# The sign of converted weights from a Prelu on ScalarE instead of a VectorE pass, and a new place for the conversions

## The chip, the cores and the metric

The kernel runs on one core of one Trainium2 chip. The core has five engines that work at the same time, each through its own instructions in order: TensorE (PE, matrix products), VectorE (DVE), ScalarE (ACT), GpSimd (POOL) and SyncE (SP, which here only starts transfers). Sixteen DMA engines move data between the chip's memory and the core's SBUF. The metric is the device time of one execution in microseconds (us). The kernel before takes 677.11 us (median of three runs, 675.74 to 677.26).

## The reference

Two stages follow each other. The first is a recurrence over time (RWKV-6 attention) on 4 sequences of 768 tokens with 8 heads of width 48; the second is a dense layer of 3072 tokens, 384 to 2048 to 384 features, with the activation h - tanh(h).

```python
for t in range(S):                      # 768 steps, per batch and head
    cur = np.einsum('bhd,bhe->bhde', u[None] * kt, vt)
    y[:, :, t] = np.einsum('bhd,bhde->bhe', rt, state + cur)
    state = wt[:, :, :, None] * state + np.einsum('bhd,bhe->bhde', kt, vt)
# ... y to (B*S, H*D) = x
h = x @ w_in
g = h - np.tanh(h)
return g @ w_out
```

The two weight matrices arrive as 64-bit floats (the division by a 64-bit root makes them so), and the kernel turns them into 32-bit floats on the chip, from the two 32-bit words of each number.

## The kernel before

The tokens are worked in eight blocks of 384. Each block's dense layer has 16 tiles of 128 features (`f` = 0 to 15): TensorE makes `hp` from `xT` and the tile's first weights, ScalarE makes six tiles from it, VectorE makes `g` from those, and three iterations later (`LAG = 3`) TensorE adds `g` times the tile's second weights to `acc`. While block i goes through its tiles, the attention of block i+1 is worked in between, a phase at a time. The attention of block 0 has nothing to hide behind; it is the "boot".

The weights are sixteen tiles as well (768 KB each as 64-bit numbers), and each must be loaded into one of five `raw` buffers and converted before its `hp`. The conversion in the kernel before has two activations on ScalarE and three passes on VectorE:

```python
UPSCALE = 2.0 ** 8
HIGH_SCALE = 2.0 ** -111
RAWS = 5                                 # buffers of the pool conv
# ...
    def load_weights(f, queue):
        raw = conv.tile([P, 2 * DM, 2], I32, name="raw", tag="raw")
        ins = queue.dma_start(out=raw, in_=weights[f].bitcast(I32).rearrange("p (n two) -> p n two", two=2))
        return f, raw, ins

    def convert(f, raw, _):
        lo, hi = raw[:, :, 0], raw[:, :, 1]
        a = w_sb[:, f, :].bitcast(I32)
        up = conv.tile([P, 2 * DM], I32, name="up", tag="up", bufs=3)
        nc.scalar.activation(out=a.bitcast(F32), in_=hi.bitcast(F32), func=AF.Copy, scale=HIGH_SCALE)   # L167
        nc.scalar.activation(out=up, in_=lo.bitcast(U32), func=AF.Copy, scale=2.0 ** -29)              # L168
        return [
            lambda: nc.vector.tensor_single_scalar(a, a, 3, op=ALU.logical_shift_left),                # L170
            lambda: nc.vector.scalar_tensor_tensor(out=a, in0=hi, scalar=-2 ** 31, in1=a,              # L171
                                                   op0=ALU.bitwise_and, op1=ALU.bitwise_or),
            lambda: nc.vector.tensor_tensor(out=a, in0=a, in1=up, op=ALU.add)]                         # L173
```

The high word, read as a 32-bit float, is scaled by 2^-111. That moves its exponent so that a shift of the bits by three to the left puts the exponent and the mantissa of the 64-bit number where a 32-bit float has them. The shift pushes the sign out, so L171 takes it from the high word again. L173 adds the upper bits of the low word.

In the boot ScalarE starts the conversions of weights 0 to 2 early. The rest of it, from the last level of the attention on, stands in this order:

```python
        converted()                                   # VectorE passes of weight 0
        for p0 in HALVES:
            blk.turn(ps, p0)                          # transposes (L340), copies ks (L342)
        for copies in last:
            copies()                                  # ScalarE copies (L328)
        begin_behind(blk.update(ps, h1), later.load("kq", kT, 0, NPAIR))   # products L358, states L369
        blk.update(ps, h2)
        ready.append(convert(*raws.pop(0)))           # weight 3 on ScalarE
        blk.result(ps, [h1, h1 + 1])                  # products L389, L407, copies to xT (L420)
        blk.fill_holes([nc.sync, nc.scalar])
        more_weights(nc.sync)                         # load of weight 5
        later.mix(0, NPAIR, ("kmix",))                # ScalarE (L220)
        blk.result(ps, [h2, h2 + 1], True)
        later.load("rp", rT, 0, NPAIR)
        converted()                                   # weight 1
        more_weights(nc.sync)                         # load of weight 6
        later.load_v()
        for _ in range(2):
            ready.append(convert(*raws.pop(0)))       # weights 4 and 5 on ScalarE
        while ready:
            converted()                               # weights 2 to 5
            if ready:
                more_weights(nc.gpsimd)               # loads of weights 7 to 9
```

During block 0 (i = 0) a plan says in which iteration each attention phase of block 1, each conversion and each load stands. The VectorE passes of a conversion come one iteration after its ScalarE part, placed between the last passes of that iteration's `g`:

```python
            steps = (1, 2, 3, 4, 5, 7, 9, 10, 12)     # level 1, 2, 4, 8, 16, 32, turn, update, result
            before = {0: ("totals 1", "totals 2", "kq")}
            behind, converted = {1: ("rp",)}, (0, 3, 4, 4, 6, 9, 9, 10, 11, 11)
            loads = {1: "weights", 2: "weights", 5: "weights", 6: "weights", 7: "weights", 8: "weights",
                     9: "rmix", 10: "kmix", 11: "wt", 13: "kq", 14: "rp", 15: "v"}
# ... the loop over the tiles of a block
        for f in range(NF):
            g, next_rest = first(here, f, ps_d)       # hp on TensorE (L467), six ScalarE steps (L474-L479)
            waiting.append((second, f, g))
            for n, op in enumerate(rest):             # VectorE: g of the tile before (L484, L489, L492)
                op()
                if n >= 2 and extra:
                    extra.pop(0)()                    # VectorE passes of conversions
            for op in extra:
                op()
            # ... attention phase of block i+1, loads
            extra = []
            for _ in range(converted.count(f)):
                extra += convert(*raws.pop(0))
            if len(waiting) > LAG:
                s, fs, gs = waiting.pop(0)
                s.add(fs, gs)                         # acc on TensorE (L505)
```

`hp` has one buffer: the product of the next tile waits until ScalarE's step h (L474) has read it. An attention level's products (L240) need the decays of kq and rp of the level before, two VectorE passes (L272).

Of the kernel before, what the change touches and what calls it, by code (L numbers as in the profile page):

```python
# [37 lines left out]
F32 = mybir.dt.float32  # L38
# [4 lines left out]
AF = mybir.ActivationFunctionType  # L43
ALU = mybir.AluOpType
# [10 lines left out]
NPAIR = H // 2  # L55
# [22 lines left out]

UPSCALE = 2.0 ** 8
HIGH_SCALE = 2.0 ** -111  # L80


@with_exitstack
def kernel(
# [10 lines left out]
    nc = tc.nc  # L95
# [58 lines left out]

    def load_weights(f, queue):
        raw = conv.tile([P, 2 * DM, 2], I32, name="raw", tag="raw")
        ins = queue.dma_start(out=raw, in_=weights[f].bitcast(I32).rearrange("p (n two) -> p n two", two=2))
        return f, raw, ins  # L160

    def convert(f, raw, _):

        lo, hi = raw[:, :, 0], raw[:, :, 1]
        a = w_sb[:, f, :].bitcast(I32)
        up = conv.tile([P, 2 * DM], I32, name="up", tag="up", bufs=3)
        nc.scalar.activation(out=a.bitcast(F32), in_=hi.bitcast(F32), func=AF.Copy, scale=HIGH_SCALE)  # L167
        nc.scalar.activation(out=up, in_=lo.bitcast(U32), func=AF.Copy, scale=2.0 ** -29)  # L168
        return [
            lambda: nc.vector.tensor_single_scalar(a, a, 3, op=ALU.logical_shift_left),  # L170
            lambda: nc.vector.scalar_tensor_tensor(out=a, in0=hi, scalar=-2 ** 31, in1=a,  # L171
                                                   op0=ALU.bitwise_and, op1=ALU.bitwise_or),
            lambda: nc.vector.tensor_tensor(out=a, in0=a, in1=up, op=ALU.add)]  # L173


# [338 lines left out]
    def plan(i):  # L514

        names = ("level 1", 2, 4, 8, 16, 32, "turn", "update", "result")
        if i == 0:

            steps = (1, 2, 3, 4, 5, 7, 9, 10, 12)
            before = {0: ("totals 1", "totals 2", "kq")}  # L520
            behind, converted = {1: ("rp",)}, (0, 3, 4, 4, 6, 9, 9, 10, 11, 11)
            loads = {1: "weights", 2: "weights", 5: "weights", 6: "weights", 7: "weights", 8: "weights",
                     9: "rmix", 10: "kmix", 11: "wt", 13: "kq", 14: "rp", 15: "v"}
        else:
            steps = (4, 5, 6, 7, 8, 9, 10, 11, 13)
            before = {0: ("kmix",), 1: ("rmix",), 2: ("totals 1",), 3: ("totals 2", "kq"), 4: ("rp",)}
            behind, converted = {}, ()
            loads = {5: "rmix", 7: "kmix", 9: "wt", 11: "kq", 14: "rp", 15: "v"}
        return dict(zip(steps, names)), before, behind, converted, loads
# [3 lines left out]
    raws = []  # L533

    def more_weights(queue):
        raws.append(load_weights(more_weights.n, queue))
        more_weights.n += 1
        return raws[-1][-1]
# [3 lines left out]
    def begin_behind(ins, dma):  # L542


        tc.add_manual_dep(dma.ins, ins.ins.name, mybir.DependencyInfo(
            mybir.DependencyClass.Sync, mybir.DependencyReason.DATA))

    def boot(ps, blk, later):

        h1, h2 = HALVES  # L550
        for p0 in HALVES:
            for name, src in (("kq", kT), ("rp", rT), ("wt", wT)):
                blk.load(name, src, p0, UP)
        for name in ("rmix", "kmix"):
            blk.tiles[name] = inp.tile([P, NPAIR * NB], F32, name=name, tag=name)
        more_weights(nc.sync)
        blk.load_v()
        for _ in range(2):
            more_weights(nc.sync)
        blk.mix(h1, UP, copy=nc.vector.tensor_copy)  # L560
        masked = blk.level_1(ps, h1)
        blk.decay(1, h1, UP)
        blk.totals(1, h1, UP)
        blk.mix(h2, UP, copy=nc.scalar.copy)
        masked()
        blk.level(ps, 2, h1, UP)
        masked = blk.level_1(ps, h2)
        blk.decay(1, h2, UP)
        blk.totals(1, h2, UP)
        for m in (2, 4, 8, 16):  # L570
            blk.totals(m, h1, UP)
        masked()
        background = [lambda: later.load("rmix", rT, 0, NPAIR), lambda: later.load("kmix", kT, 0, NPAIR),
                      lambda: later.load("wt", wT, 0, NPAIR)] + [lambda: more_weights(nc.sync)] * 2
        ready, last = [], []
        for m in (2, 4, 8, 16, 32):
            for p0 in HALVES:
                if (m, p0) != (2, h1):
                    ins = blk.level(ps, m, p0, UP, last)
                if p0 == h2 or m == 32:  # L580
                    blk.totals(m, p0, UP)
            begin_behind(ins, background.pop(0)())
            if m <= 8:
                ready.append(convert(*raws.pop(0)))
            if m == 8:
                later.mix(0, NPAIR, ("rmix",))

        def converted():
            for op in ready.pop(0):
                op()  # L590

        converted()
        for p0 in HALVES:
            blk.turn(ps, p0)
        for copies in last:
            copies()
        begin_behind(blk.update(ps, h1), later.load("kq", kT, 0, NPAIR))
        blk.update(ps, h2)
        ready.append(convert(*raws.pop(0)))
        blk.result(ps, [h1, h1 + 1])  # L600
        blk.fill_holes([nc.sync, nc.scalar])
        more_weights(nc.sync)
        later.mix(0, NPAIR, ("kmix",))
        blk.result(ps, [h2, h2 + 1], True)
        later.load("rp", rT, 0, NPAIR)
        converted()
        more_weights(nc.sync)
        later.load_v()
        for _ in range(2):
            ready.append(convert(*raws.pop(0)))  # L610
        while ready:
            converted()
            if ready:
                more_weights(nc.gpsimd)

    with tc.tile_pool(name="ps_boot", bufs=4, space=PSUM) as ps_boot:
        xT = blocks[0].begin()
        boot(ps_boot, blocks[0], blocks[1])
# [3 lines left out]
    for i, blk in enumerate(blocks):  # L622
        here = xT
        later = blocks[i + 1] if i + 1 < len(blocks) else None
        after = blocks[i + 2] if i + 2 < len(blocks) else None
        if later:
            xT = later.begin()
        phases, before, behind, converted, loads = plan(i)
        second = Second(blk.b * S + blk.q * NB, ps_d)
        for f in range(NF):  # L630
# [82 lines left out]
```

## Time and profile before

| what | value |
|---|---|
| time, median of 3 | 677.11 us |
| span of the profiled execution | 677.3 us |
| TensorE busy | 642.3 us (95%) |
| VectorE busy | 559.3 us (83%) |
| ScalarE busy | 488.7 us (72%) |
| conversions, ScalarE (L167, L168) | 14.6 and 14.6 us for 16 each |
| conversions, VectorE (L170, L171, L173) | 9.0, 15.3 and 15.2 us for 16 each |
| loads of raw weights | 13 by SyncE, 3 by GpSimd, 768 KB each |

The busy shares are averages over the whole span. The conversions all lie in the first 126 us of it: the VectorE pass L171 has its first start at 30.6 us and its last at 124.9 us. The profile also has a view of windows, which gives the busy time of each engine in a stretch:

```profile
40.00:50.00 10.00, 7.06 (x59) 3.98 (x58) 8.80 (x11) 7.94 (x15) 1.74 (x3) 0.56 0.84 306
50.00:60.00 10.00, 4.97 (x104) 3.15 (x103) 8.38 (x17) 5.84 (x12) 0.00 (x0) 0.78 0.82 324
130.00:140.00 10.00, 10.00 (x32) 5.89 (x31) 9.38 (x19) 7.72 (x16) 0.00 (x0) 1.00 0.43 156
```

Each line has a stretch and its length, then the busy time of TensorE, of its weight loads, of VectorE, ScalarE and GpSimd with the number of instructions, the granted TensorE clock as a share of full speed, the DMA engines' busy share and the GB/s they moved. In 50 to 60 us TensorE is busy for half the time and its clock is on average at 0.78; in 130 to 140 us it has no gap at all.

### The profile page before, as it was taken

The numbers are of one execution on the slowest core, as the hardware profiler recorded it, in microseconds if no ns is written. First come the engines' busy times: TensorE is split into PE (matmuls) and PEld (weight loads), VectorE is DVE, ScalarE is ACT, GpSimd is POOL, SyncE is SP. The second block draws the span as 40 slices with busy tenths as digits, with TensorE's granted clock in tenths as the row PEclk, the third lists the DMA queues.
The fourth block names the chain that finished last, engine by engine and source line by source line (L and its number), as shares of the span: only waits on it lengthen the run. The fifth ranks groups of instructions, "written<-read, shape, count | busy, mean of one in ns | idle before, by whom it ended". The sixth has DMA issues, their size and how long they took to land.

```text
span 677.3 us, 19991 instructions
## 1 busy us (share of the span) xinstructions
PE 642.3 (95%) x8480; PEld 411.3 (61%) x8480; DVE 559.3 (83%) x1117; ACT 488.7 (72%) x966; POOL 5.2 (1%) x20
## 2 busy tenths in 40 slices
PE   4866899999999999999999999999999999999997
PEld 4743566566665666656666666656666566655554
DVE  7898999999986997689985998769986899747664
ACT  4575889885777758686676858677577857768874
POOL 2010000000000000000000000000000000000000
PEclk9967999999999999999999999999999999999999
DMA  8775152404012401124012130025011200000000
GB/s 311 236 253 215 49 179 104 137 36 143 5 47 90 147 32 49 24 94 150 3 47 92 39 140 23 28 90 176 4 48 49 79 2 3 3 10 35 1 1 36
DMA packets 30842, 54.38 MB, mean 80 GB/s; under 512 B 2336, under 2 KB 28704, under 8 KB 30752
## 3 DMA queue, kind: packets, MB, share of 16 engines
q1 hardware_dynamic: 30080, 50.46, 22.0%
q0 software_dynamic: 432, 2.36, 0.8%
q8 instruction: 67, 1.10, 0.7%
q10 hardware_dynamic: 240, 0.27, 0.1%
q14 instruction: 23, 0.19, 0.1%
HBM read 47.19 MB, written 4.72 MB: 77 GB/s over the span
## 4 chain that ended last, share of the span: by engine, by line
PE 71%; DVE 14%; issue 4%; PEld 4%; DMA 3%; ACT 3%; PEldq 1%; SPq 0%; DVEq 0%
PE acc L505 31%; PE hp L467 28%; PE att L240 8%; DVE states L369 2%; DMA raw<-in_weights 2%; PE att L407 2%; DVE hs L484 2%; PE att L340 2%; PEld hp L467 2%; PEld att L389 1%; DVE rp L272 1%; DVE gT L484 1%; DVE kq L272 1%; DVE w_sb L173 1%; DVE gT L492 1%
## 5 line engine op out<-in xcount | busy, mean ns | idle before, releaser
L467 PE MATMUL hp<-xT,w_sb 128*128 128x384 f32 x768 | 273.2, 493 | 8.9 <-ACT h L474 5.7
L505 PE MATMUL acc<-w_sb,gT 128*128 128x384 f32 x768 | 273.8, 493 | 0.0
L467 PEld LDWEIGHTS hp<-xT,w_sb 128*128 128x128 f32 x768 | 147.0, 192 | 113.0 <-ACT h L474 7.0
L505 PEld LDWEIGHTS acc<-w_sb,gT 128*128 128x128 f32 x768 | 140.5, 190 | 88.7 <-ACT o L510 2.3
L474 ACT ACTIVATE h<-hp 128x384 f32<-128x384 f32 x128 | 62.7, 490 | 144.9 <-PE hp L467 144.3
L489 DVE TENSOR_TENSOR th<-h,th 128x384 f32<-128x384 f32 x128 | 70.8, 553 | 43.9 <-ACT th L478 43.9
L484 DVE SCALAR_TENSOR_TENSOR hs<-h,s 128x384 f32<-128x384 f32 x128 | 70.9, 554 | 25.7 <-ACT s L475 25.7
L492 DVE COPY_PREDICATED gT<-big,th 128x384 f32<-128x384 int32 x128 | 76.1, 595 | 12.5
L476 ACT ACTIVATE qa<-s,shift 128x384 f32<-128x384 f32 x128 | 78.8, 615 | 4.2
L484 DVE SCALAR_TENSOR_TENSOR gT<-qb,hs 128x384 f32<-128x384 f32 x128 | 71.4, 558 | 9.4
L479 ACT ACTIVATE big<-s,shift 128x384 f32<-128x384 f32 x128 | 76.8, 600 | 0.0
L477 ACT ACTIVATE qb<-s,shift 128x384 f32<-128x384 f32 x128 | 76.7, 600 | 0.0
L484 DVE SCALAR_TENSOR_TENSOR hs<-qa,hs 128x384 f32<-128x384 f32 x128 | 70.4, 550 | 0.0
L475 ACT ACTIVATE s<-h 128x384 f32<-128x384 f32 x128 | 67.0, 523 | 4.1
L240 PEld LDWEIGHTS att<-rp,kq 48*64 48x64 f32 x3072 | 53.5, 145 | 25.1 <-issue 13.3
L240 PE MATMUL att<-rp,kq 48*64 48x32 f32 x3072 | 57.3, 229 | 8.1 <-DVE rp L272 5.5
L478 ACT ACTIVATE th<-h 128x384 f32<-128x384 f32 x128 | 64.9, 507 | 0.0
L272 DVE TENSOR_TENSOR kq<-kq,tot 128x768 f32<-128x768 f32 (+1 forms) x45 | 38.6, 858 | 4.0 <-PE att L240 2.6
L272 DVE TENSOR_TENSOR rp<-rp,tot 128x768 f32<-128x768 f32 (+1 forms) x45 | 38.8, 862 | 0.0
L369 DVE SCALAR_TENSOR_TENSOR states<-states,tot,att 128x48 f32<-128x48 f32 x176 | 31.5, 258 | 6.1 <-PE att L358 6.1
L300 DVE COPY_PREDICATED scores<-mask_all,att 128x384 f32<-128x384 uint8 (+1 forms) x54 | 31.9, 657 | 0.0
L240 PE MATMUL att<-rmix,kmix 48*64 48x64 f32 x768 | 14.5, 232 | 6.9 <-ACT rmix L220 6.9
(55 smaller groups left out, 352.1 us busy)
## 6 DMA issues: line engine op xcount, KB each, us to landing
raw<-in_weights SPq DMA_DIRECT2D x13, 768.0 KB, 4.6
rmix<-in_rT SPq DMA_DIRECT2D x7, 768.0 KB, 5.2
kmix<-in_kT SPq DMA_DIRECT2D x7, 768.0 KB, 6.8
wt<-in_wT SPq DMA_DIRECT2D x7, 768.0 KB, 7.7
kq<-in_kT SPq DMA_DIRECT2D x7, 768.0 KB, 4.5
rp<-in_rT SPq DMA_DIRECT2D x7, 768.0 KB, 4.7
v_sb<-in_v SPq DMA_DIRECT2D x8, 576.0 KB, 5.6
out_y<-o SPq DMA_DIRECT2D x23, 192.0 KB, 1.9
```

Of the source, the lines that this page charges most:

```text
L240: nc.tensor.matmul(dst, lhsT=lhs[rows, t0:t0 + L], rhs=src, start=True, stop=True)
L272: ins = nc.vector.tensor_tensor(out=part, in0=part, in1=by, op=ALU.mult)
L467: nc.tensor.matmul(hp, lhsT=w_in_sb[:, f, kc, :], rhs=xT[:, kc, :], start=(kc == KC - 1), stop=(kc == 0))
L475: nc.scalar.activation(out=s, in_=h, func=AF.Square)
L476: nc.scalar.activation(out=qa, in_=s, func=AF.Square, bias=shift[:, 0:1])
L477: nc.scalar.activation(out=qb, in_=s, func=AF.Square, bias=shift[:, 1:2])
L478: nc.scalar.activation(out=th, in_=h, func=AF.Tanh)
L479: nc.scalar.activation(out=big, in_=s, func=AF.Relu, bias=shift[:, 2:3])
L484: return lambda: nc.vector.scalar_tensor_tensor(out=out, in0=in0, scalar=scalar, in1=in1, op0=op0, op1=ALU.mult)
L489: lambda: nc.vector.tensor_tensor(out=th, in0=h, in1=th, op=ALU.subtract),
L492: lambda: nc.vector.copy_predicated(out=g, mask=big.bitcast(I32), data=th)]
L505: nc.tensor.matmul(acc, lhsT=g[:, j * P:(j + 1) * P], rhs=w_out_sb[:, f, :], start=(f == 0), stop=(f == NF - 1))
```

## The change

The sign comes from ScalarE. The first activation of a conversion becomes a Prelu with slope -2^32 for negative inputs: a positive number goes through as before; a negative one comes out positive and 2^32 times larger. That is a change of 32 in the exponent field, and the shift by three to the left carries this bit into the place of the sign. VectorE's pass L171 is left out. So VectorE no longer reads the raw words: a raw buffer is free when ScalarE's two activations have read it.

The conversions move too. In the boot the VectorE passes of weight 0 stand behind the updates of the state instead of ahead of them, weight 3 is converted after the transfers into the holes of xT, and the scaling of kmix moves ahead of the updates. Weights 7 to 10 are loaded in the boot by SyncE (7 to 9 were loaded by GpSimd, 10 in block 0). In block 0 the attention phases from level 16 on stand one iteration later, and the conversions are spread anew.

```diff
+NEGATIVE = -2.0 ** 32
...
-        nc.scalar.activation(out=a.bitcast(F32), in_=hi.bitcast(F32), func=AF.Copy, scale=HIGH_SCALE)
+        nc.scalar.activation(out=a.bitcast(F32), in_=hi.bitcast(F32), func=AF.Prelu,
+                             scale=HIGH_SCALE, alpha=NEGATIVE)
...
             lambda: nc.vector.tensor_single_scalar(a, a, 3, op=ALU.logical_shift_left),
-            lambda: nc.vector.scalar_tensor_tensor(out=a, in0=hi, scalar=-2 ** 31, in1=a,
-                                                   op0=ALU.bitwise_and, op1=ALU.bitwise_or),
             lambda: nc.vector.tensor_tensor(out=a, in0=a, in1=up, op=ALU.add)]
...
-            steps = (1, 2, 3, 4, 5, 7, 9, 10, 12)
+            steps = (1, 2, 3, 4, 6, 8, 10, 11, 13)
-            behind, converted = {1: ("rp",)}, (0, 3, 4, 4, 6, 9, 9, 10, 11, 11)
-            loads = {1: "weights", 2: "weights", 5: "weights", 6: "weights", 7: "weights", 8: "weights",
+            behind, converted = {1: ("rp",)}, (0, 3, 3, 4, 4, 6, 10, 10, 12, 13)
+            loads = {2: "weights", 5: "weights", 6: "weights", 7: "weights", 8: "weights",
...
-        converted()
         for p0 in HALVES:
             blk.turn(ps, p0)
         for copies in last:
             copies()
+        later.mix(0, NPAIR, ("kmix",))
         begin_behind(blk.update(ps, h1), later.load("kq", kT, 0, NPAIR))
         blk.update(ps, h2)
-        ready.append(convert(*raws.pop(0)))
         blk.result(ps, [h1, h1 + 1])
         blk.fill_holes([nc.sync, nc.scalar])
+        converted()
+        ready.append(convert(*raws.pop(0)))
         more_weights(nc.sync)
-        later.mix(0, NPAIR, ("kmix",))
+        converted()
         blk.result(ps, [h2, h2 + 1], True)
         later.load("rp", rT, 0, NPAIR)
-        converted()
         more_weights(nc.sync)
         later.load_v()
         for _ in range(2):
             ready.append(convert(*raws.pop(0)))
         while ready:
             converted()
-            if ready:
-                more_weights(nc.gpsimd)
+            more_weights(nc.sync)
```

## The prediction

> **What bounds the kernel now.** I read the busy shares first, then the forty slices, then the chain of waits of the first 72 us, and last the timelines of TensorE, ScalarE and VectorE there. TensorE is busy 95% of the span. From 118.60 us to the end it is busy 550.98 of 558.70 us, so nothing that ends after 118.60 us can give much, and the change touches nothing there. Before 118.60 us TensorE has gaps, and all sixteen weight conversions lie there: six of their VectorE parts before 50 us, ten between 56 and 125 us. The chain of waits shows what sets the pace in the middle of this stretch (start, length, what):
>
> ```profile
> 42.04 13.77 DMA raw<-in_weights
> 55.81 0.02 issue
> 55.84 0.90 ACT w_sb L167
> ...
> 57.79 0.87 DVE w_sb L171
> 58.66 0.06 DVE gT L492
> 58.72 0.33 issue
> 59.05 0.95 DVE w_sb L173
> 60.00 1.82 DVE scores L247 x2
> 61.82 0.84 DVE rp L272
> ```
>
> A weight load issued at 42.04 us lands 13.77 us later. ScalarE, which works in order, sits in front of the conversion of weight 6 until then, and the step h of the next dense tile stands behind it. Then VectorE carries the chain, with the sign pass (L171) in it. TensorE's timeline shows the price in brackets:
>
> ```profile
> 44.32 4.21 PE L467 MATMUL hp<-xT,w_sb 128*128 128x384 f32 x6 [2.19 <-ACT xT L420]
> 49.17 2.20 PE L467 MATMUL hp<-xT,w_sb 128*128 128x384 f32 x6 [0.64 <-ACT h L474]
> 51.30 1.63 PE L240 MATMUL att<-rmix,kmix 48*64 48x64 f32 x96
> 57.95 4.21 PE L467 MATMUL hp<-xT,w_sb 128*128 128x384 f32 x6 [5.03 <-ACT h L474]
> 62.76 1.60 PE L240 MATMUL att<-rp,kq 48*64 48x32 f32 x96 [0.60 <-PE hp L467]
> 64.29 2.20 PE L467 MATMUL hp<-xT,w_sb 128*128 128x384 f32 x6
> 67.20 1.60 PE L240 MATMUL att<-rp,kq 48*64 48x32 f32 x96 [0.71 <-DVE rp L272]
> ...
> 73.31 1.60 PE L240 MATMUL att<-rp,kq 48*64 48x32 f32 x96 [0.45 <-DVE rp L272]
> ...
> 80.53 1.60 PE L240 MATMUL att<-rp,kq 48*64 48x32 f32 x96 [1.55 <-DVE rp L272]
> ...
> 90.44 1.01 PE L317 MATMUL att<-rp,kq 48*32 48x32 f32 x96 [0.37 <-DVE rp L272]
> ...
> 109.34 2.17 PE L467 MATMUL hp<-xT,w_sb 128*128 128x384 f32 x6 [1.09 <-ACT qb L477]
> ```
>
> Each dense tile's hp is six records. It takes 2.1 to 2.2 us at the full clock and 4.21 us at the half clock. From the first second-layer product, at 68.73 us, to 118.60 us the gaps are 0.45 + 1.55 + 0.37 + 1.09 = 3.46 us. In 60 to 120 us VectorE is busy 98%: it is the bound of block 0, TensorE a close second. The pieces of a conversion (mean ns after the comma):
>
> ```profile
> L171 DVE SCALAR_TENSOR_TENSOR w_sb<-raw,w_sb 128x768 int32<-128x768 int32 x16 | 15.3, 956 | 0.3
> L173 DVE CUSTOM_DVE_ANT_0 w_sb<-w_sb,up 128x1536 uint16<-128x1536 uint16 x16 | 15.2, 952 | 1.2
> L167 ACT ACTIVATE w_sb<-raw 128x768 f32<-128x768 f32 x16 | 14.6, 911 | 7.9 <-DMA raw<-in_weights 7.8
> L170 DVE TENSOR_SCALAR w_sb<-w_sb 128x768 int32<-128x768 int32 x16 | 9.0, 560 | 2.0 <-ACT w_sb L167 2.0
> ```
>
> [...] So Prelu should take the 911 ns of Copy. The trace agrees for its other functions of one form (h 490, th 507, s 523 ns at 384 columns), and the built program of the change has, like the kernel before, one table load (1283 ns in the trace, at 0.82 us)[...]. [...] idle from 52.93 us, the clock reads 0.91 in 54 to 56 us and 0.50 in 56 to 62 us. [...] three loads issued by GpSimd at 41.55, 44.15 and 47.33 us share the engines with those of SyncE, and a 768 KB SyncE load takes 13.77 us here against a median of 4.6 us.
>
> **The change part by part.** (a) It removes sixteen L171 passes. Started back to back, an instruction costs its spacing and not its duration: in the boot the conversions follow each other every 2.55 us (36.82, 39.37, 41.93), and without L171 it should be 1.5 us (0.59 from shift to next, then 0.87). Inside block 0 an L171 costs 0.87 us when interleaved, 1.1 us in a bare sequence. So six times 1.05 = 6.3 us in the boot and ten times about 0.9 = 9 us in block 0 leave VectorE. Most of it cannot be cashed in, so I follow the path.
>
> (b) The first conversion moves from ahead of the state updates to behind them. It lay at 30.02 to 32.6 us, and the first update began at 32.61 us. But TensorE's update products start only at 31.54 us and their first half needs 0.9 us, so updates begin no earlier: 0 us. The end of the updates stays at 36.8 us.
>
> (c) On ScalarE the kmix scaling (1.56 us) and the conversion of weight 3 (1.7 us) change places. The second group of xT copies, which releases the first hp, starts about 0.2 us later, so hp starts at about 44.55 us for 44.32 us: +0.2 us. It is again at the half clock, ending at 48.75 us.
>
> (d) VectorE's boot conversions now wait for ScalarE. ScalarE gives weight 3 at 42.6 us and, after the xT copies, 4 and 5 at 46.2 and 47.8 us. VectorE ends the last at 48.7 us instead of 50.35 us, though 6.3 us of work is gone: it idles for the rest. Then totals (2.61 us), the kq decay (0.87 us) and the first dense chain, from 52.2 us instead of 53.83 us.
>
> (e) The loads of weights 7 to 9 move from GpSimd to SyncE, behind weight 6. Ahead of weight 6 are then only weight 5 and rp. Three 0.786 MB loads at the 0.40 to 0.43 MB/us seen between 46 and 56 us take 5.5 to 6 us from 42 us[...]. ScalarE finishes tile 0's six steps at 51.9 us, so it converts weight 6 at once instead of at 55.84 us. A raw buffer is also free after ScalarE's two reads, so no later load waits for VectorE.
>
> (f) Then h of tile 1 is at 53.55 us instead of 57.43 us, and hp of tile 2 at 54.05 us instead of 57.95 us. TensorE has then been idle about 1.1 us, not 5, so it should stay at the full clock. VectorE: dense chain 0 with the two conversion passes from 52.2 to 55.9 us, L247 to 57.7 us, rp decay to 58.55 us; chain 1 starts there and not at 62.57 us. Adding 2.4 us for chain 1 and 1.74 us for the level 2 decays gives 62.7 us, when the products that began at 67.20 us can begin; the first second-layer product follows at 64.4 us instead of 68.73 us: **4.3 us** gained.
>
> (g) After that, by iteration of block 0 (PE: hp 1.95, acc 1.95, attention 1.0 to 1.7; VectorE: chain 2.35, conversion 1.33, decays 1.74, masked copy 0.93). Iterations 4 and 5 carry two conversions each, 7.7 and 5.0 us of VectorE work against 5.6 and 4.0 us of TensorE work, but the two iterations after them have slack and level 16 and 32 moved one later, to 6 and 8. I find the decays of level 4 done at 68.5 us, when TensorE arrives, and those of level 8 at 76.2 us against an arrival at 78.1 us. ScalarE, with two conversions (3.25 us) in 3, 4 and 10, arrives in time by 0.1 to 0.6 us. So TensorE should become the bound, and the 3.46 us of gaps go: **3.5 us**. Sum 7.8 us; I keep 0.2 us for new small gaps. 677.1 - 7.6 = **669.5 us**.
>
> **The rivals.** *VectorE sets everything:* all 15 us off a nearly full engine would come off the time, 662 us. Against it: (d) leaves VectorE waiting for ScalarE, and TensorE's own idle time from 57.95 to 118.60 us is 60.65 - 55.78 = 4.9 us; with the 3.9 us of (f) and 2.1 us of half clock the ceiling is about 11 us. *Nothing reaches the end:* if weight 6 still lands late, since the same bytes cross the same engines, (f) fails and only the 3.5 us and part of 1.6 us remain: 673 us. Against it stands the order of the loads; for it, the 13.77 us. *ScalarE takes over:* it is busy 98% in 100 to 120 us and the change takes nothing from it. If Prelu cost 0.1 us more, or the two conversions at 10 delay h, gaps of 1 to 2 us come back: 671 us. *The clock drops again:* TensorE waits some 2.4 us at 56.1 us for the rp decay; if that makes it cold, hp costs 2.1 us more: 671.5 us.
>
> **Range and chances.** The rivals that cost lie 1.5 to 3.5 us above 669.5 us, the ones that gain are limited by 11 us, that is 666 us. Range 667 to 672.5 us. A gain of over 2% needs under 663.6 us, below the ceiling: 0.03. A loss of 2% would need a new wait of 20 us: 0.01. Within 2%: 0.96.
>
> **What would show it.** The L171 group gone and the conversion activation still near 911 ns; no wait for the load before weight 6 and hp of tile 2 near 54 us at 2.1 us; the first L505 product near 64.4 us; the bracketed gaps of L240 after it under 0.3 us; after 118.6 us nothing but a shift. It is wrong if ScalarE still waits for weight 6, if hp of tile 2 takes 4.2 us, or if waits for h of over 1 us appear in iterations 10 to 14.

## The result and the profile after

| | median | range | runs |
|---|---|---|---|
| before | 677.18 us | 675.74 to 677.65 us | 4 |
| after | 671.54 us | 671.01 to 673.00 us | 4 |

The ratio is 0.9924 with a 95% interval of 0.9902 to 0.9945: 5.6 us less, inside the 2% that counts as the same. Measured again later beside other kernels, the changed kernel had 672.34 us against 676.99 us, a ratio of 0.9931 (0.9917 to 0.9945). The prediction was 669.5 us, range 667.0 to 672.5 us. The profiled execution has a span of 669.7 us; VectorE's busy time went from 559.3 to 545.4 us, ScalarE's from 488.7 to 488.8 us. Lines of the kernel after lie two or three below those of before: hp is L469, the first conversion activation L170.

The chain of waits of the kernel after, in the stretch where before a weight load of 13.77 us stood:

```profile
50.58 0.51 ACT big L481
51.09 0.83 ACT w_sb L170
...
53.15 2.22 PE hp L469 x6
55.36 2.62 issue
57.98 2.79 PE att L242 x96
60.77 3.87 PE hp L469 x6
```

No transfer stands ahead of the conversion of weight 6 any more: ScalarE goes from the last step of tile 0 (`big`) straight into it, and hp of tile 2 starts at 53.15 us for 57.95 us. But further down there is a hole of 2.62 us, then an attention product of 2.79 us and an hp of 3.87 us. TensorE's timeline over the same time:

```profile
53.15 2.20 PE L469 MATMUL hp<-xT,w_sb 128*128 128x384 f32 x6 [0.88 <-ACT h L476]
57.98 2.79 PE L242 MATMUL att<-rp,kq 48*64 48x32 f32 x96 [2.63 <-issue]
60.70 3.94 PE L469 MATMUL hp<-xT,w_sb 128*128 128x384 f32 x6
64.58 1.60 PE L242 MATMUL att<-rp,kq 48*64 48x32 f32 x96
66.11 2.20 PE L507 MATMUL acc<-w_sb,gT 128*128 128x384 f32 x6
...
70.17 1.60 PE L242 MATMUL att<-rp,kq 48*64 48x32 f32 x96
...
117.09 0.36 PE L409 MATMUL att<-scores,v_sb 64*48 64x64 f32 x9 [0.74 <-issue]
```

The first second-layer product starts at 66.11 us (68.73 us before), and from there to 120 us only one gap of 0.74 us is left of 3.46 us; the product at 70.17 us, for example, waits for nothing. The windows of the kernel after give the granted clock (third number from the end) beside the busy times:

```profile
56.00:58.00 2.00, 0.02 (x3) 0.05 (x3) 2.00 (x4) 1.94 (x5) 0.00 (x0) 0.86 0.98 412
58.00:60.00 2.00, 2.00 (x76) 2.00 (x80) 1.86 (x5) 0.72 (x2) 0.00 (x0) 0.50 0.17 64
...
62.00:64.00 2.00, 2.00 (x4) 1.01 (x3) 2.00 (x3) 0.00 (x0) 0.00 (x0) 0.50 0.00 0
64.00:66.00 2.00, 2.00 (x98) 1.43 (x96) 1.97 (x5) 1.25 (x3) 0.00 (x0) 0.94 0.03 8
```

The clock falls inside the hole and comes back only at about 64.2 us (an estimate from the 0.94, with the half clock before and the full clock after): what runs between takes longer, the attention product 2.79 us for 1.60 us and hp of tile 3 3.94 us for 2.20 us. VectorE's timeline says what the hole waited for, which the chain calls "issue":

```profile
32.48 4.29 DVE L371 SCALAR_TENSOR_TENSOR states<-states,tot,att 128x48 f32<-128x48 f32 x24 [3.05 <-PE att L360]
...
44.72 0.56 DVE L174 TENSOR_SCALAR w_sb<-w_sb 128x768 int32<-128x768 int32 x1 [1.68 <-ACT w_sb L170]
...
56.94 0.94 DVE L274 TENSOR_TENSOR rp<-rp,wt 128x768 f32<-128x768 f32 x1
...
61.70 0.95 DVE L274 TENSOR_TENSOR rp<-rp,tot 128x768 f32<-128x768 f32 x1
```

The rp decay ends at 57.88 us and the product starts at 57.98 us. The next decay ends at 62.65 us; its product starts at 64.58 us, when TensorE at half clock has got there. The groups of the conversion:

```profile
L172 ACT ACTIVATE up<-raw 128x768 int32<-128x768 uint32 x16 | 14.7, 917 | 0.0
L170 ACT ACTIVATE w_sb<-raw 128x768 f32<-128x768 f32 x16 | 14.6, 911 | 7.0 <-DMA raw<-in_weights 4.1 <-issue 2.7
```

The Prelu (L170) takes 911 ns, to the nanosecond what the Copy took. Comparing the start of every hp in both traces gives the balance: tile 2 is 4.80 us earlier, tile 4 2.62 us, the end of block 0 5.15 us. Between that point and the last products some 1.1 us more come from small stalls, and 1.4 us of the 7.6 us between the two spans lie in the last store; that these two parts belong to the change is not shown.

### The profile page after: what moved, and what is told of

Read it like the earlier page. It is cut to its first block, busy times and chain, and to the rows that moved or that the text cites. A ratio compares the mean times of both kernels' runs of the same rounds, so it can differ in the third digit from the quotient of the medians.

```text
span 669.7 us, 19951 instructions
## 1 busy us (share of the span) xinstructions
PE 642.5 (96%) x8480; PEld 412.5 (62%) x8480; DVE 545.4 (81%) x1101; ACT 488.8 (73%) x966; POOL 3.5 (1%) x17
## 4 chain that ended last, share of the span: by engine, by line
PE 81%; PEld 4%; issue 4%; DVE 4%; ACT 3%; DMA 2%; PEldq 1%; SPq 0%; ACTq 0%; DVEq 0%
PE acc L507 34%; PE hp L469 33%; PE att L242 9%; DVE states L371 2%; PE att L409 2%; PEld hp L469 2%; PE att L342 2%; PEld att L391 2%; PE att L319 1%; PEld acc L507 1%; DMA wt<-in_wT 1%; DMA xT<-late 1%; PEldq L397 0%; ACT qb L479 0%; ACT h L476 0%
## 5 line engine op out<-in xcount | busy, mean ns | idle before, releaser
L469 PE MATMUL hp<-xT,w_sb 128*128 128x384 f32 x768 | 272.4, 492 | 4.0 <-DMA xT<-late 2.5
L469 PEld LDWEIGHTS hp<-xT,w_sb 128*128 128x128 f32 x768 | 147.0, 192 | 107.7 <-ACT h L476 3.4
L476 ACT ACTIVATE h<-hp 128x384 f32<-128x384 f32 x128 | 62.7, 490 | 143.5 <-PE hp L469 142.8
L242 PE MATMUL att<-rp,kq 48*64 48x32 f32 x3072 | 58.8, 231 | 6.5 <-issue 4.4
L274 DVE TENSOR_TENSOR kq<-kq,tot 128x768 f32<-128x768 f32 (+1 forms) x45 | 38.6, 859 | 4.2 <-PE att L242 2.3
L274 DVE TENSOR_TENSOR rp<-rp,tot 128x768 f32<-128x768 f32 (+1 forms) x45 | 38.8, 862 | 0.0
```

What stands on the lines that cost most here:

```text
L242: nc.tensor.matmul(dst, lhsT=lhs[rows, t0:t0 + L], rhs=src, start=True, stop=True)
L274: ins = nc.vector.tensor_tensor(out=part, in0=part, in1=by, op=ALU.mult)
L469: nc.tensor.matmul(hp, lhsT=w_in_sb[:, f, kc, :], rhs=xT[:, kc, :], start=(kc == KC - 1), stop=(kc == 0))
```

## The experiments

Three questions: is it the Prelu or the new order that pays; is the half clock after 57.4 us what was lost against the prediction; and is there more to be had once that is gone. None of these kernels leaves out a part of the computation.

| kernel | median us | before, same batch | ratio (95%) |
|---|---|---|---|
| Prelu alone | 673.48 | 677.57 | 0.9934 (0.9915 to 0.9954) |
| order and loads alone | 681.75 | 677.57 | 1.0062 (1.0043 to 1.0082) |
| after, loads by GpSimd | 674.83 | 677.57 | 0.9950 (0.9932 to 0.9969) |
| after, four fillers | 671.24 | 677.57 | 0.9902 (0.9882 to 0.9921) |
| after, conversions spread | 671.94 | 676.90 | 0.9916 (0.9891 to 0.9941) |
| after, totals into the hole | 670.07 | 676.90 | 0.9889 (0.9861 to 0.9916) |
| spread, totals, two fillers | 670.22 | 676.90 | 0.9886 (0.9862 to 0.9910) |
| the same, holes of xT by one queue | 670.03 | 676.90 | 0.9884 (0.9858 to 0.9911) |
| after again | 672.34 | 676.99 | 0.9931 (0.9917 to 0.9945) |
| after, fillers in two places | 670.67 | 676.99 | 0.9904 (0.9888 to 0.9920) |
| all together | 670.35 | 676.99 | 0.9897 (0.9879 to 0.9916) |
| after, weight 0 placed back | 672.37 | 676.99 | 0.9930 (0.9915 to 0.9944) |

**The Prelu alone.** The kernel before with only the conversion changed:

```diff
-  ... in_=hi, func=AF.Copy, scale=HIGH_SCALE)
+  ... in_=hi, func=AF.Prelu, scale=HIGH_SCALE, alpha=NEGATIVE)
-  lambda: nc.vector.scalar_tensor_tensor(out=a, in0=hi, scalar=-2 ** 31, ...)
```

> The kernel before with only the sign moved to Prelu and the VectorE pass left out; order, plan and loads as before. Theory A (a raw buffer is free as soon as ScalarE has read it, so weight 6 need not share the engines with three late loads, and VectorE has 15 us less to do; the new order adds little): weight 6 is there before 52 us, the gaps of TensorE after 66 us shrink, 671 to 673 us. Rival B (the new order of the boot and of block 0 and the loads on SyncE bring the gain, the pass was hidden): ScalarE still waits 3 to 4 us for weight 6, 675 to 677 us.

Measured: 673.48 us, 0.9934, half a us above the range of theory A; the ratios of the whole change (0.9924 and 0.9931) lie inside this interval, so that the new order and loads add anything is not shown. In the traces hp of tile 15 starts at 122.61 us here, 123.30 us in the kernel after and 128.44 us before. One reason is in GpSimd's timeline. First the kernel before, then the one with the Prelu alone; both issue the same three loads:

```profile
41.55 0.69 POOL L159 DMA_DIRECT2D raw<-in_weights  x1 [37.37 <-DVE w_sb L171]
44.15 0.53 POOL L159 DMA_DIRECT2D raw<-in_weights  x1 [1.91 <-DVE w_sb L171]
47.33 0.53 POOL L159 DMA_DIRECT2D raw<-in_weights  x1 [2.65 <-ACT w_sb L167]
```

```profile
20.63 0.69 POOL L160 DMA_DIRECT2D raw<-in_weights  x1 [16.45 <-ACT up L170]
36.87 0.53 POOL L160 DMA_DIRECT2D raw<-in_weights  x1 [15.55 <-ACT up L170]
46.64 0.53 POOL L160 DMA_DIRECT2D raw<-in_weights  x1 [9.24 <-ACT up L170]
```

Before, a raw buffer was free only when VectorE's L171 had read it, so the three loads were issued within 6 us, just when weight 6 was wanted. Without L171 ScalarE's second activation frees it; two of the three loads go out before 37 us. The conversion of weight 6 then starts with no wait for its load, though queue and order are those of before and that load itself is issued later, at 43.90 us for 42.04 us. ScalarE's timeline:

```profile
52.13 0.90 ACT L168 ACTIVATE w_sb<-raw 128x768 f32<-128x768 f32 x1
```

The other reason is VectorE's shorter work: its boot conversions end at 49.02 us for 50.35 us, and the level 2 decays at 63.31 us for 67.05 us. No run has the one without the other, so the share of each stays open. TensorE of this kernel, too, loses its clock (0.72 in 60 to 62 us, 0.50 in 62 to 64 us), and its timeline shows it:

```profile
59.02 1.60 PE L240 MATMUL att<-rp,kq 48*64 48x32 f32 x96 [1.37 <-issue]
60.55 3.90 PE L467 MATMUL hp<-xT,w_sb 128*128 128x384 f32 x6
```

**The order and loads alone.** The changed kernel with Copy and L171 put back.

> The changed kernel with the old conversion: Copy and the VectorE pass back, the new order, plan and loads kept. Theory A: VectorE is the bound again and its six boot conversions (2.55 us each) start at 36.7 us, so they end about 52 us instead of 48 us; everything after is later, 677 to 680 us, no better than before. Rival B: the order and the loads carry the gain, 671 to 673 us.

Measured: 681.75 us, slower by 0.62% (0.43 to 0.82) and above the 677 to 680 us of theory A. Weight 6 comes in time here too, although VectorE's L171 still reads the raw buffers: the new order of the loads is enough for that by itself. But VectorE, with all six conversions of the boot behind the updates and 2.56 us for each, is late. One line of ScalarE's, one of TensorE's and two of VectorE's timeline in this kernel:

```profile
51.83 0.89 ACT L170 ACTIVATE w_sb<-raw 128x768 f32<-128x768 f32 x1
```

```profile
63.14 2.78 PE L243 MATMUL att<-rp,kq 48*64 48x32 f32 x96 [6.10 <-issue]
```

```profile
52.29 0.95 DVE L261 TENSOR_TENSOR tot<-wt 128x768 f32<-128x768 f32 x1
...
62.10 0.94 DVE L275 TENSOR_TENSOR rp<-rp,wt 128x768 f32<-128x768 f32 x1
```

The totals, which follow the last boot conversion, start at 52.29 us (47.99 us in the kernel after), and the rp decay, 5.2 us later than in the kernel after, holds the product at 63.14 us. The order is one that only the short conversion can bear; by itself it costs 4.2 us.

**GpSimd loads weights 7 to 10.** The changed kernel with one word changed:

```diff
             converted()
-            more_weights(nc.sync)
+            more_weights(nc.gpsimd)
```

> The changed kernel with the loads of weights 7 to 10 issued by GpSimd. Theory A: with the raw buffers free early, weight 7 is loaded before 30 us already and weight 6 shares with one load only; it lands by 51 us, 671 to 672.5 us, the same as the change. Rival C (taking the loads out of the second queue is what made weight 6 early): weight 6 lands after 54 us, 674 to 676 us.

Measured: 674.83 us, in the range of rival C; the ratio is 0.9950 (0.9932 to 0.9969), which overlaps the changed kernel's 0.9931 (0.9917 to 0.9945); that the queue costs something is not shown. In the trace the conversion of weight 6 waits 0.48 us for its load, at 53.6 us, not 4 us: this lies between the 51 us of theory A and the 54 us of rival C. Once the buffers are free early, the queue is worth half a microsecond there. In this profile the first hp starts at 45.73 us, 1.5 us later than in the kernel after.

**Filler products.** Four products into the banks of `acc`, overwritten later, ahead of the attention phase of iteration 2, so that TensorE does not stand idle while VectorE ends the rp decay:

```diff
+                if i == 0 and f == 2:
+                    second.warm(here, 4)          # 4 x matmul(acc[k % 3], 128x128, 128x384)
                 for name in before.get(f, ()):
                     later.prepare(name)
```

> The changed kernel with four extra products (2.7 us at the full clock, their result is overwritten) between hp of tile 2 and the level 2 products, where TensorE is idle from 55.4 to 58.0 us. Theory D (this idle time drops the clock, and the attention products of 2.79 us and the hp of 3.94 us that follow cost 1.8 us net): both return to 1.6 and 2.2 us, the first second-layer product starts 1.5 to 2 us earlier, 669.5 to 670.2 us. Rival E (VectorE's decays set that product anyway): 671.5 us.

TensorE's timeline of this kernel (L510 is the filler):

```profile
55.27 2.20 PE L469 MATMUL hp<-xT,w_sb 128*128 128x384 f32 x6 [0.87 <-ACT h L476]
57.31 2.74 PE L510 MATMUL acc<-xT,w_sb 128*128 128x384 f32 x8
59.99 1.60 PE L242 MATMUL att<-rp,kq 48*64 48x32 f32 x96
61.52 2.20 PE L469 MATMUL hp<-xT,w_sb 128*128 128x384 f32 x6
64.40 1.60 PE L242 MATMUL att<-rp,kq 48*64 48x32 f32 x96 [0.68 <-DVE rp L274]
65.93 2.20 PE L516 MATMUL acc<-w_sb,gT 128*128 128x384 f32 x6
```

With work that computes nothing the clock stays full (1.00 in every window from 52 to 68 us), hp of tile 3 takes 2.20 us, and from hp of tile 2 to the first second-layer product it is 10.66 us instead of 12.96 us. That is the cause of the loss in this stretch, shown. The 2.3 us are not all kept: the product at 64.40 us now waits 0.68 us for VectorE's decay, and from hp of tile 2 to hp of tile 15 it is 68.38 us instead of 70.15 us. In this profile the boot came out later (first hp at 45.77 us for 44.24 us), which hides the gain in the span. The time, 671.24 us, is what rival E expected, not the 669.5 to 670.2 us of theory D, whose signs in the trace all came; the ratio 0.9902 doesn't part this kernel from the changed one.

**Fillers in two places.** The same, and three more products ahead of the first hp, in one batch with the changed kernel.

```diff
         blk.result(ps, [h2, h2 + 1], True)
+        filler = scratch(ps)
+        for _ in range(3):
+            nc.tensor.matmul(filler[:, 0, 0:DM], lhsT=w_in_sb[:, 0, 0, :], rhs=w_out_sb[:, 0, :], ...)
```

> The changed kernel once more, beside the three others of this batch, as their reference: 671.5 us, between 670.5 and 672.5 us. Its profile should show the hp product of tile 3 at close to 3.9 us and the first second-layer product some 2.6 us earlier than in the kernel before, counted from the first hp.

> The changed kernel with four filler products ahead of the first dense attention (as in the run with fillers before) and three more ahead of the first hp of the boot. Clock theory (TensorE is at the half clock only because it had too little to do just before): the first hp takes about 3 us or less instead of 3.6 to 4.2, the second 2.2 us, and the hp of tile 3 2.2 us, so the first second-layer product comes 2.3 to 3.3 us earlier than in the changed kernel and the time is 668 to 670 us. VectorE theory (block 0 is bound by VectorE once the clock is full, and takes back what TensorE gains): hp products are short, but the end of block 0 moves by under 1 us and the time is 671 to 672 us.

Measured: 670.67 us against 672.34 us, and all four runs with fillers (670.11 to 671.58 us) lie below all six without (671.93 to 673.92 us): some 1.7 us. So the fillers are worth something in the time, too; 670.67 us lies between the ranges of the two theories. In the changed kernel hp of tile 3 takes 4.18 us this time, and the first second-layer product, counted from the first hp, comes 1.9 us earlier than in the kernel before (22.54 us for 24.41 us), not the 2.6 us expected. In the profiled executions the fillers of the boot have no part in the gain. TensorE's timeline (L619 is the boot's filler):

```profile
41.77 3.75 PE L619 MATMUL att<-w_sb 128*128 128x384 f32 x6
45.62 2.21 PE L469 MATMUL hp<-xT,w_sb 128*128 128x384 f32 x6
48.63 2.20 PE L469 MATMUL hp<-xT,w_sb 128*128 128x384 f32 x6 [0.80 <-ACT h L476]
```

They take 3.75 us themselves, where hp's six products of this size take 2.20 us at the full clock. The first hp is then short, 2.21 us, but starts at 45.62 us; in the changed kernel of the same batch it starts at 43.67 us and takes 4.10 us. Both end at about 47.8 us, and the second hp starts at 48.63 us here and 48.41 us there. What the fillers of iteration 2 save is kept down by VectorE: the gaps `[0.71 <-DVE rp L274]` and `[0.45 <-DVE rp L274]` stand at 63.44 and 69.56 us.

**Weight 0 placed back.** The changed kernel with VectorE's conversion of weight 0 ahead of the updates again, as it was before.

> The changed kernel with VectorE's conversion of weight 0 moved back ahead of the state updates, and nothing else. Theory of the prediction (that pass fits into a hole in which VectorE waits for TensorE, and after the updates VectorE waits for ScalarE's weights 4 and 5 anyway): no difference, 670.5 to 672.5 us, update start within 0.5 us of 32.5 us, VectorE's wait for ScalarE longer by about 1.5 us. Rival (the new place of the first conversion carries part of the gain): updates and the first hp start 1 us or more later and the time is 672.5 to 674 us.

Measured: 672.37 us against 672.34 us. VectorE's timeline:

```profile
32.15 4.29 DVE L371 SCALAR_TENSOR_TENSOR states<-states,tot,att 128x48 f32<-128x48 f32 x24 [1.47 <-PE att L360]
...
40.85 0.56 DVE L174 TENSOR_SCALAR w_sb<-w_sb 128x768 int32<-128x768 int32 x1 [1.27 <-ACT w_sb L170]
...
44.68 0.56 DVE L174 TENSOR_SCALAR w_sb<-w_sb 128x768 int32<-128x768 int32 x1 [2.06 <-ACT w_sb L170]
```

The conversion fills half of the hole ahead of the updates (1.47 us of wait instead of 3.05 us), and what it gains is waited off again later, 1.27 and 2.06 us, for ScalarE's weights. The place of that conversion is worth nothing either way.

**Is there more?** If the hole ahead of the updates is free, it can take work that stands later on the path: the totals of the next block (2.61 us), needed before the kq decay.

```diff
+        for m in (1, 2, 4, 8, 16):
+            later.totals(m, 0, NPAIR)
         for p0 in HALVES:
             blk.turn(ps, p0)
...
         blk.update(ps, h2)
+        later.totals(32, 0, NPAIR)
...
-            before = {0: ("totals 1", "totals 2", "kq")}
+            before = {0: ("kq",)}
```

> The changed kernel with 2.4 us of VectorE work of block 1 (its totals but the last) moved into the 3.0 us in which VectorE waits at 29.4 us, the place that the conversion of weight 0 left. Theory F: the first dense chain is limited by ScalarE's th of tile 0 at 50.6 us and by weight 6 instead, so about 1.1 us of the 2.4 us is gained, 670 to 670.8 us. Rival G: 671.5 us. If the totals wait for their load and hold up the updates: 672 us or more.

Measured: 670.07 us, 0.9889 (0.9861 to 0.9916), as theory F expected and the largest gain so far. Its interval overlaps the changed kernel's first one (0.9902 to 0.9945) and just misses the second (0.9917 to 0.9945), so the trace has to speak. TensorE's timeline:

```profile
53.68 2.20 PE L469 MATMUL hp<-xT,w_sb 128*128 128x384 f32 x6 [0.89 <-ACT h L476]
57.60 1.60 PE L242 MATMUL att<-rp,kq 48*64 48x32 f32 x96 [1.72 <-issue]
59.13 2.20 PE L469 MATMUL hp<-xT,w_sb 128*128 128x384 f32 x6
62.04 1.62 PE L242 MATMUL att<-rp,kq 48*64 48x32 f32 x96 [0.71 <-DVE rp L274]
63.59 2.20 PE L507 MATMUL acc<-w_sb,gT 128*128 128x384 f32 x6
```

The wait for the rp decay is 1.72 us instead of 2.63 us, the clock stays at 1.00 from 50 to 66 us, and hp of tile 3 takes 2.20 us with no filler. That is one execution, with a mean clock of 0.995 over its span. One other of the six has 0.995 too; the other four have 0.990 to 0.992, so TensorE had the full clock for less of the span in them, and their median is 670.6 us against 669.8 us of these two. The changed kernel has 0.982 to 0.990 in its ten executions. How much of the gain is the earlier decay and how much the clock is therefore not shown. The conversions spread otherwise, the plan of block 0 being

```diff
-  converted = (0, 3, 3, 4, 4, 6, 10, 10, 12, 13);  loads = {2: "weights", 5: ...
+  converted = (3, 3, 4, 4, 6, 7, 10, 10, 12, 13);  loads = {4: "weights", 5: ...
```

> The changed kernel with the conversion of weight 6 moved from iteration 0 to 3 and the next ones one place on (3, 3, 4, 4, 6, 7, 10, 10, 12, 13). Theory F (from 44 to 66 us VectorE's chain sets when the first second-layer product starts, not TensorE): 1.3 us of VectorE work and 1.6 us of ScalarE work leave that stretch, the product starts 1.3 us earlier or a little more if the clock then holds, 669.5 to 670.5 us. Rival G (TensorE is the bound from there on and the gain is spent already): 671.5 us, no difference from the change.

gave 671.94 us, 0.9916, no difference from the changed kernel, as rival G said: hp of tile 3 still took 3.56 us after a wait of 2.40 us. Then the pieces were put together: both edits and two fillers; the same with the holes of xT filled by SyncE alone and weight 4 converted earlier; and this with the boot's fillers added.

> Both of these moves together, and two extra products (1.35 us, overwritten) between hp of tile 2 and the level 2 products to hold the clock. Theory F: with weight 6 out of the way VectorE reaches the level 2 decays at about 59.3 us instead of 62.65 us, the first second-layer product starts near 61 us instead of 66.1 us, 665.5 to 667.5 us. Rival G: 670 to 671 us, the clock's part alone.

> As the run before, and the transfers into the holes of xT all issued by SyncE, which frees ScalarE of 3 us of issuing at 37 us, with the conversion of weight 4 brought forward into this time. Theory F: VectorE's boot conversions end 1 to 1.6 us earlier and so does what hangs on them, 664.5 to 666.5 us. If the holes land later than with two queues (hp of tile 0 waits for them at 44.1 us in the change), hp of tile 0 starts 1 us later and the gain is gone, 666 to 668 us.

> All that helped together: totals of the next block in VectorE's hole of the boot, conversions of block 0 spread anew, xT's holes filled by one queue, filler products ahead of the dense attention (two) and ahead of the first hp (three). If the pieces add up, the first hp is warm and the time is 668 to 669.5 us. If VectorE and ScalarE take turns in setting block 0, one piece is worth as much as all of them, and the time stays at 670 us like the version with the totals alone.

They gave 670.22, 670.03 and 670.35 us. The 665.5 to 667.5 us and 664.5 to 666.5 us of theory F were missed by some 3 us and more, and none is better than the totals alone. The version with one queue has its first second-layer product at 63.07 us, 0.5 us ahead of the totals alone, but hp of tile 15 starts at 120.87 us in both profiles: block 0's later gaps, 0.46 us at 93.59 us for ScalarE's h and 1.01 us of "issue" at 114.60 us, take the rest. In the third, the boot's fillers take 4.21 us and the first hp starts only at 47.31 us. 670 us was reached from three sides and not passed; the totals in the hole, a gain of 7 us on the kernel before, is the one to keep.

## Why the prediction was right, and where it was not

The time fell inside the range, 2 us above the predicted value, at the value of the rival *the clock drops again* (671.5 us). That the value fits so well is in part luck: this rival counted 2.1 us for hp alone, while step (f) lost 1.7 us and step (g) 0.8 us, and some of that came back behind block 0, where nothing was predicted (5.6 us in the time, 5.15 us by the end of block 0).

(a) Held: the L171 group is gone and the Prelu costs 911 ns, the time of the Copy, as the author had estimated; the trace after has one table load, as before (1283 ns). VectorE's busy time fell by 13.9 us (some 15 us said), and, as said, most of that reached no end of the path.

(b) Held: moved back, weight 0's conversion made 0.0 us of difference. The updates ended at 36.7 us (36.8 us said).

(c) The date held, 44.24 us for the first hp in this profile (44.55 us said), at half clock at first (0.50 in 44 to 46 us), but the reason did not, so this is luck. The second group of xT copies starts 0.5 us earlier than before (42.36 us there), not 0.2 us later, and the first hp waits for a transfer into the holes of xT instead:

```profile
41.84 1.93 ACT L422 COPY xT<-att 48x384 f32<-48x384 f32 x4
44.24 3.63 PE L469 MATMUL hp<-xT,w_sb 128*128 128x384 f32 x6 [2.45 <-DMA xT<-late]
```

Its start scatters between 43.67 and 46.12 us over the profiles of kernels without fillers in the boot, more than the 0.2 us that this step speaks of.

(d) Held: VectorE waits for weights 4 and 5 and ends its boot conversions at 47.99 us (48.7 us said); the dense chain starts at 51.47 us (52.2 us said).

(e) The dates held: weight 6 is converted at 50.99 us with no wait (51.9 us said). The cause named, the order of the loads, is enough: with the order alone the wait is gone. But so is the freed raw buffer, a remark at the end of this step: with the Prelu alone, queue and order as before, the wait is gone too, and with GpSimd's queue in the new order 0.48 us is left of it. Either removes it, and the step gave nearly all the weight to one.

(f) Is the step that failed, by one term. hp of tile 2 at 53.15 us (54.05 us), chain 1 from 57.80 us (58.55 us), the level 2 decays done at 62.65 us (62.7 us): VectorE's side came out to 0.1 us. But the products did not begin then. The step took TensorE to "stay at the full clock" after its idle time of 1.1 us, which it did (0.88 us of idle time, a clock of 1.00 from 52 to 56 us, hp of tile 2 at 2.20 us), and then passed over the second wait, of 2.4 us, which only the rival counted. That TensorE could stand idle so long and keep its clock was the author's estimate. The trace before held a warning: with the full clock of 52 to 54 us (1.00) until the drop and the half clock of 56 to 58 us (0.50) after it, the 0.91 in 54 to 56 us puts the drop, by estimate, at 55.6 us, 2.7 us after TensorE went idle at 52.93 us. The second wait measured 2.63 us, the attention product 2.79 us for 1.60 us, hp of tile 3 3.94 us for 2.1 us, and TensorE reached the next product 1.9 us after its decays. The first second-layer product came at 66.11 us, not 64.4 us: 2.6 us gained, not 4.3 us. The fillers show that the clock is the cause: with them it is 10.66 us from hp of tile 2 to the first second-layer product, against 10.35 us by the prediction's dates and 12.96 us in the kernel after.

(g) Right in kind, a little too large: gaps of 3.46 us became 0.74 us. From the first second-layer product to the end of block 0 that is 5.15 - 2.62 = 2.5 us where 3.3 us were counted.

The rival *ScalarE takes over* did not come: TensorE waits for no h in iterations 10 to 14. *Nothing reaches the end* and *VectorE sets everything* are ruled out by the missing wait for weight 6 and by the two waits for ScalarE in the boot.

## What to carry to other kernels

Removing a pass does not pay by its own length (15.3 us of L171 here for a gain of 4 to 6 us), so ask what waits for it and what it holds: this one stood in the chain of waits and was the last reader of a load buffer, and so set the time at which the next loads start. When a gain leaves TensorE idle on the path, price the clock as part of the path, not as a rival: here, after 2.63 us of idle time, the next hp took 3.94 us for 2.20 us. Look for the hole that a change opens elsewhere and put there what stands on the path: the same operations in another place gave about as much as filler work did.

## What was not expected of the hardware

The length of TensorE's idle time did not by itself say whether the clock fell. In the kernel after, the mean clock of 0.70 in 46 to 48 us, 0.86 in 56 to 58 us and 0.94 in 64 to 66 us puts the changes at 47.2, 57.4 and 64.2 us, the drop 2.1 us after the last product. These dates are estimates from the window means, with the clock at 1.00 on one side of a change and at 0.50 on the other, as the windows beside them read. With the Prelu alone (0.98 in 54 to 56, 0.72 in 60 to 62 and 0.92 in 64 to 66 us) the changes stand by the same estimate at 54.1, 60.9 and 64.3 us. The drop there comes while TensorE is busy: hp of tile 3 has started at 60.55 us, and the idle time of 1.37 us ended at 59.02 us.

| kernel | TensorE idle | hp of tile 1 | hp of tile 3 |
|---|---|---|---|
| after | 2.63 us | 2.20 us | 3.94 us |
| Prelu alone | 1.37 us | 4.21 us | 3.90 us |
| weight 0 placed back | 1.54 us | 4.21 us | 3.90 us |
| loads by GpSimd | 1.59 us | 4.05 us | 3.65 us |
| totals into the hole | 1.72 us | 2.20 us | 2.20 us |

In three kernels an idle time of 1.37 to 1.59 us and then 1.60 to 1.78 us of attention products stood ahead of an hp of tile 3 of 3.65 to 3.90 us; in a fourth, 1.72 us and then 1.60 us stood ahead of one of 2.20 us. What decides between them was not shown. On the way back, in the kernel after, TensorE had work without a gap from 57.98 us on, first 2.79 us of attention products and then hp of tile 3, and the clock was full again only at 64.2 us, 6.2 us later.
